# Top-k attention with a gated feed-forward on one core: the first eight units moved to a three-stage order with folded scores

## The chip, the cores and the metric

The kernel runs on one core of one Trainium2 chip. Its time is the device time of one execution in microseconds (us), the median of several runs. Five engines of the core matter here. PE is TensorE, the matrix engine (PEld is its loading of weights). DVE is VectorE, ACT is ScalarE, POOL is GpSimd. SP is the queue from which nearly all transfers are issued. Each engine works through its own instructions in program order and waits on the others through semaphores.

## The reference

There are 8 batches of 8 heads, 576 tokens and 64 elements per head. For each query only the 32 largest scores are kept. The result is put together to 4608 rows of 512, which go through a feed-forward with 2048 hidden elements.

```python
def _attn_ref(q, k, v):                       # q, k, v: (8, 8, 576, 64)
    scores = 1.0 / np.sqrt(D) * np.matmul(q, k.transpose(0, 1, 3, 2))
    kth = np.partition(scores, -32, axis=-1)[..., -32:-31]
    scores = np.where(scores >= kth, scores, -1000000000.0)
    scores = scores - np.max(scores, axis=-1, keepdims=True)
    attn = np.exp(scores)
    attn = attn / (np.sum(attn, axis=-1, keepdims=True) + 1e-09)
    return np.matmul(attn, v)

def _moe_ref(x, w_in, w_out):                 # w_in: (512, 2048), w_out: (2048, 512)
    h = x @ w_in
    g = h * np.cos(h)
    return g @ w_out
```

The two weight matrices arrive as 64-bit floats and the kernel turns them into 32-bit floats itself. This is called decoding here.

## The kernel before

The attention is cut into 144 units: 128 tokens and a pair of heads each. Four units in a row (the four pairs of heads) make a block of 128 tokens, ready for the feed-forward. The program is a loop over slots. In slot i unit i is searched for its 32 largest scores, while older units are at later stages. Weights come in 32 chunks of 512 KB: 16 of w_in, then 16 of w_out.

A chunk goes from a transfer to ACT, then to DVE, then to POOL:

```python
def decode_first(n):      # ACT: abs, sign, low word
    ...
        nc.scalar.activation(out=w, in_=hi.bitcast(F32), func=AF.Abs, scale=2.0**16)
        nc.scalar.sign(hi.bitcast(F32), hi)
        nc.scalar.mul(out=lo, in_=lo.bitcast(U32), mul=2.0**-29)
def decode_second(n):     # DVE: maximum, shift
    ...
        nc.vector.tensor_scalar(out=w, in0=w, scalar1=2.0, scalar2=None, op0=ALU.max)
        nc.vector.tensor_scalar(out=wi, in0=wi, scalar1=3, scalar2=None, op0=ALU.logical_shift_left)
def decode_third():       # POOL: add the low word, multiply by the sign
    ...
        nc.gpsimd.tensor_tensor(out=wi, in0=wi, in1=st[:, :, 0], op=ALU.add)
        nc.gpsimd.tensor_tensor(out=w, in0=w, in1=st[:, :, 1].bitcast(F32), op=ALU.mult)
```

A new chunk is loaded only while fewer than 8 chunks and live feed-forward tiles are held (`staged() + ff["live"] >= CHUNKS` stops it).

The search of a unit has two forms. Without folding, each of four rounds takes the eight largest of 576 scores for two heads (`max`), and three rounds remove them (`match_replace`). With folding, the scores are first split into the larger and the smaller of two halves (288 each). The larger halves get four rounds, the smaller ones two, and two small reductions in the next slot merge the results:

```python
def fold(u, op):                      # op is max, then min
    ...
    nc.vector.tensor_tensor(out=u["rest"][...], in0=sc[:, :, 0, 0:HS], in1=s[:, :, HS:S], op=op)
def topk_round(u, rnd):
    ...
    if u["folds"]:
        search(at, rest[:, :, 0:HS], rest[:, :, 0:HS], rnd < lasts)
        if rnd < TOPK // 16:
            search(low, rest[:, :, HS:S], rest[:, :, HS:S], rnd < TOPK // 16 - 1)
    else:
        search(at, u["s"] if rnd == 0 else rest, rest, rnd < lasts)
```

`sc` is the tile in PSUM in which `scores` leaves a unit's scores. There is one (`bufs=1`), and `transposes_now` uses the same. `take_scores` copies it to `s` on ACT.

The later stages: `bounds`, `mask` and `exponentials` (ACT), `reciprocal` (DVE), `normalise` (POOL), the transposes (on PE in the early slots, and then copied by ACT; by transfers later), `values` (PE) and `take_values` (ACT). The feed-forward runs beside them: `feed(n)` issues up to n steps on PE. A step needs credit (4.1 a slot, at most 5), finished values or gated tiles that are two ticks old (each `feed` is a tick), and decoded weights. `take_banks` copies finished PSUM banks (ACT). `reduce_first` and `reduce_second` reduce the argument of the cosine (POOL), `sines` evaluates it (ACT), `gate` multiplies (POOL).

The early slots are these:

```python
EARLY, LAST = 2 * NP, NU - NP         # 8, 140
u["folds"] = EARLY + 2 <= i < LAST + 2

def early_slot(i, u, w):              # u = unit i, w = unit i - 1
    n = 3 if i < 6 else 2
    topk_first(u, w)                  # merges of w, folds or first round of u
    decode_second(1 if i == 0 else n)
    scores(units[i + 1])
    for load, b, hp in at_slot.get(i, []):
        load(b, hp)
    load_weights(n)
    if w:
        bounds(w)
        mask(w)
        exponentials(w)
        reciprocal(w)
    topk_round(u, 1)
    if i == 0:
        decode_second(2)
    topk_round(u, 2)
    topk_round(u, 3)
    if w:
        normalise(w)
    take_banks()
    take_scores(units[i + 1])
    gate(1)
    decode_third()
    feed(2)
    reduce_first()
    reduce_second()
    if i != NP:
        decode_first(n - 1)
    if w:
        transposes_now(w)
    feed(1)
    decode_first(n - len(wq["second"]))
    if w:
        values([w])
        take_values([w])
    feed(2)
    sines(2)
```

`sines(2)` evaluates when two reduced tiles wait, or one has waited long enough. Slots 0 to 8 are such early slots; slots 9 to 140 have another order (`slot`), with the search first, then `decode_second(2)`, and with normalise, split, write and a transfer that transposes for units two and three slots old. The last four have an order of their own.

Of the kernel before, what the change touches and what calls it, by code (L numbers as in the profile page):

```python
# [31 lines left out]
def kernel(  # L32
# [16 lines left out]
    NP = H // 2  # L49
# [35 lines left out]
    for i in range(DF // CW):  # L85
        w = consts.tile([P, NC, CW], F32, tag=f"w_in{i}", name=f"w_in{i}")
# [16 lines left out]
    def load_weights(n):  # L103
        for _ in range(n):
            i = wq["next"]
            if i >= len(chunks):
                return
            src, dst = chunks[i]
            if not DECODE:
                nc.sync.dma_start(out=dst, in_=src)  # L110
                wq["next"] = wq["done"] = i + 1
                continue
            if staged() + ff["live"] >= CHUNKS:
                return
            st = ffw.tile([P, CW, 2], I32, tag="g", name="st", bufs=CHUNKS)
            nc.sync.dma_start(out=st.rearrange("p w i -> p (w i)"), in_=src)
            wq["loaded"].append((st, dst))
            wq["next"] = i + 1
# [87 lines left out]
    def scores(u):  # L206
        sc = u["sc"] = ps.tile([P, 2, 2, 512], F32, tag="sc", name="sc", bufs=1)
        for h in range(2):
            for j in range(2):
                d = slice(j * D, (j + 1) * D)  # L210
                for b, q0, rows, r0 in u["parts"]:
                    st = pairs[b, u["hp"]]
                    nc.tensor.matmul(  # L213
                        sc[r0 : r0 + rows, j, h, 0:HS],
                        st["q"][d, q0 : q0 + rows],
                        st["k"][d, h * HS : (h + 1) * HS],
                        start=True,
                        stop=True,
                    )

    def take_scores(u):
        s = u["s"] = work.tile([P, 2, S], F32, tag="s", name="s", bufs=4)
        nc.scalar.copy(  # L223
            out=s.rearrange("p j (h w) -> p (j h) w", h=2),
            in_=u["sc"].rearrange("p j h w -> p (j h) w")[:, :, 0:HS],
        )
        if not u["folds"]:
            del u["sc"]
# [23 lines left out]
    def topk_first(u, w):  # L252

        u["top"] = tops[u["n"] % len(tops)]
        merges = [merge_first, merge_second] if w and w["folds"] else []
        if u["folds"]:
            for op in (ALU.max, ALU.min):
                fold(u, op)
                if merges:
                    merges.pop(0)(w)  # L260
        else:
            u["rest"] = work.tile([P, 2, S], F32, tag="rest", name="rest", bufs=1)
        for merge in merges:
            merge(w)
        topk_round(u, 0)
# [38 lines left out]
    def bounds(u):  # L304

        ends = u.pop("top").rearrange("p j r i -> p j (r i)")
        ends = ends[:, :, 2 * TOPK - 2 :] if u["folds"] else ends[:, :, 2 * TOPK - 2 :: 2 - 2 * TOPK]
        nb = u["nb"] = small.tile([P, 2, 2], F32, tag="nb", name="nb")
        nc.scalar.mul(out=nb, in_=ends, mul=-SCALE)  # L309
        nd = u["nd"] = small.tile([P, 2], F32, tag="nd", name="nd")  # L310
        for j in range(2):
            nc.scalar.activation(  # L312
                out=nd[:, j : j + 1], in_=ends[:, j, 1:2], func=AF.Identity,
                bias=nb[:, j, 0:1], scale=SCALE,
            )

    def mask(u):

        s, nb = u["s"], u.pop("nb")
        for j in range(2):  # L320
            nc.scalar.activation(  # L321
                out=s[:, j], in_=s[:, j], func=AF.Prelu, bias=nb[:, j, 1:2], scale=SCALE, alpha=FAR
            )

    def exponentials(u):
        s, nd = u["s"], u.pop("nd")
        den = u["den"] = small.tile([P, 2], F32, tag="den", name="den")
        for j in range(2):
            nc.scalar.activation(  # L329
                out=s[:, j], in_=s[:, j], func=AF.Exp, bias=nd[:, j : j + 1], scale=1.0,  # L330
                accum_out=den[:, j : j + 1],
            )

        nc.scalar.activation(out=den, in_=den, func=AF.Identity, bias=eps, scale=1.0)

    def reciprocal(u):
        u["rden"] = small.tile([P, 2], F32, tag="rden", name="rden")
        nc.vector.reciprocal(u["rden"], u.pop("den"))  # L338

    def normalise(u):  # L340
        s, rden = u["s"], u.pop("rden")
        for j in range(2):
            nc.gpsimd.tensor_scalar(  # L343
                out=s[:, j], in0=s[:, j], scalar1=rden[:, j : j + 1], scalar2=1.0,
                op0=ALU.mult, op1=ALU.mult,
            )
# [123 lines left out]
    def take_banks():  # L470
        while full:
            take, *what = full.popleft()
            take(*what)
# [122 lines left out]

    EARLY, LAST = 2 * NP, NU - NP

    for i, u in enumerate(units):
        u["n"] = i
        u["folds"] = EARLY + 2 <= i < LAST + 2

    def early_slot(i, u, w):
        n = 3 if i < 6 else 2
        topk_first(u, w)
        decode_second(1 if i == 0 else n)
        scores(units[i + 1])
        for load, b, hp in at_slot.get(i, []):  # L610
            load(b, hp)
        load_weights(n)
        if w:
            bounds(w)
            mask(w)
            exponentials(w)
            reciprocal(w)
        topk_round(u, 1)
        if i == 0:
            decode_second(2)  # L620
        topk_round(u, 2)
        topk_round(u, 3)
        if w:
            normalise(w)
        take_banks()
        take_scores(units[i + 1])
        gate(1)
        decode_third()
        feed(2)
        reduce_first()  # L630
        reduce_second()
        if i != NP:
            decode_first(n - 1)
        if w:
            transposes_now(w)
        feed(1)
        decode_first(n - len(wq["second"]))
        if w:
            values([w])
            take_values([w])  # L640
        feed(2)
        sines(2)

    def slot(i, u, w, x, y, z):
        if x:
# [94 lines left out]
    for i in range(NU + 1):  # L740
        ff["end"] = i >= NU
        ff["credit"] = min(ff["credit"] + 4.1, 5.0)
        ff["now"] += 1
        wq["ready"] = wq["done"]
        u, w = (units[i - n] if 0 <= i - n < NU else None for n in range(2))
        x, y = (units[i - n] if EARLY <= i - n < LAST else None for n in range(2, 4))
        z = units[i - 5 : i - 3] if i % 2 and EARLY <= i - 5 < LAST else None
        if i <= EARLY:
            early_slot(i, u, w)
        elif i <= LAST:  # L750
            slot(i, u, w, x, y, z)
        else:
            last_slot(i, u, w, x, y, z)
# [47 lines left out]
```

## Time and profile before

| | before |
|---|---|
| time, median of 3 runs | 1527.04 us (1526.19 to 1527.17) |
| span of the profiled execution | 1522.8 us |
| PE busy | 1433.9 us (94%) |
| DVE busy | 1417.3 us (93%) |
| POOL busy | 1107.0 us (73%) |
| ACT busy | 1069.3 us (70%) |
| start of slots 0, 1, 6, 10, 15 | 7.94, 21.37, 86.24, 139.98, 195.98 us |

The profile is that of one execution. A line of it names the source line (L138), the engine, the operation, what it writes and reads, the shape, how often it came, its busy time and the mean duration in ns. After the last bar stands the idle time before it and what ended that. The view of stretches has the length of each stretch and then the busy time of each engine in it. The timeline has a start, a duration and one or several merged instructions per line. The start of a slot is read from the timeline as the first DVE instruction of its unit.

### The profile page before, as it was taken

How to read it: one execution, taken by the hardware profiler on the slowest of the kernel's cores; microseconds unless marked ns; L12 is line 12 of the kernel's file. 1: busy time of each engine (PE TensorE's matmuls, PEld its weight loads, DVE VectorE, ACT ScalarE, POOL GpSimd, SP SyncE). 2: the span in 40 equal slices, each digit the busy share in tenths (PEclk: the TensorE clock that was granted, in tenths of full speed). 3: DMA queues.
4: the chain of work that ended last, by engine and by line, in shares of the span. 5: the costliest groups of instructions: out<-in, count | busy, mean ns of one | idle time of the engine just before them, and what ended most of it. 6: DMA issues, size and time to landing. Idle time of an engine off the chain costs nothing.

```text
span 1522.8 us, 30130 instructions
## 1 busy us (share of the span) xinstructions
PE 1433.9 (94%) x10360; PEld 1023.1 (67%) x10360; DVE 1417.3 (93%) x4689; ACT 1069.3 (70%) x2120; POOL 1107.0 (73%) x838
## 2 busy tenths in 40 slices
PE   4577798999999999999999999999999999999998
PEld 3464466676767676767676767676767676767575
DVE  7999999999999999999999999999999999999721
ACT  7888667676767677767676777676777777776731
POOL 4777958777878787878787878777777777787600
PEclk6688899999999999999999999999999999999999
DMA  8432365536664655554665455645554456544200
GB/s 271 141 93 83 96 169 166 163 117 160 170 165 111 152 144 165 161 148 137 165 171 138 126 148 165 177 121 159 164 163 132 133 142 167 139 141 114 70 10 14
DMA packets 371754, 212.20 MB, mean 139 GB/s; under 512 B 321296, under 2 KB 337937, under 8 KB 371601
## 3 DMA queue, kind: packets, MB, share of 16 engines
q1 hardware_dynamic: 366192, 200.63, 48.0%
q10 hardware_dynamic: 5408, 9.65, 1.8%
q8 instruction: 81, 1.33, 0.4%
q14 instruction: 73, 0.59, 0.1%
HBM read 45.09 MB, written 87.29 MB: 87 GB/s over the span
## 4 chain that ended last, share of the span: by engine, by line
PE 70%; ACT 13%; DVE 10%; DMA 3%; issue 2%; SPq 1%; POOL 0%; ACTq 0%; POOLq 0%; DVEq 0%
PE mm L454 30%; PE o L530 23%; PE sc L213 8%; PE o L404 8%; DVE top L299 4%; DVE rest L302 3%; ACT s L329 2%; ACT x L511 2%; ACT s L321 2%; DMA pT<-rows 2%; ACT s L223 1%; ACT L511 1%; DVE rest L239 1%; DVE w_out L138 1%; ACT nd L312 1%
## 5 line engine op out<-in xcount | busy, mean ns | idle before, releaser
L299 DVE MAX8 top<-rest 128x8 f32<-128x288 f32 (+1 forms) x1656 | 682.2, 461 | 0.0
L454 PEld LDWEIGHTS mm<-xT,w_in 128*128 128x128 f32 x4608 | 545.0, 193 | 102.2 <-issue 91.8
L454 PE MATMUL mm<-xT,w_in 128*128 128x128 f32 x4608 | 565.2, 278 | 4.3 <-ACT xT L410 4.2
L530 PE MATMUL o<-w_out,g 128*128 128x512 f32 x1152 | 541.8, 603 | 4.0 <-POOL w_out L148 3.9
L302 DVE MATCH_REPLACE8 rest<-top,rest 128x288 f32<-128x288 f32 (+1 forms) x1104 | 495.5, 457 | 0.0
L530 PEld LDWEIGHTS o<-w_out,g 128*128 128x128 f32 x1152 | 203.8, 192 | 201.2 <-issue 193.0
L343 POOL TENSOR_SCALAR s<-s,rden 128x576 f32<-128x576 f32 x288 | 212.9, 751 | 139.3 <-DVE rden L338 139.3
L355 POOL COPY halves<-s 128x2304 uint16<-128x2304 uint16 x132 | 277.8, 2105 | 35.6 <-DMA rows<-halves 28.5
L329 ACT ACTIVATE s<-s,nd 128x576 f32<-128x576 f32 x288 | 220.7, 769 | 0.4
L223 ACT COPY s<-sc 128x1152 f32<-128x1152 f32 x144 | 160.7, 1116 | 84.9 <-PE sc L213 84.7
L321 ACT ACTIVATE s<-s,nb 128x576 f32<-128x576 f32 x288 | 205.4, 760 | 0.0
L213 PE MATMUL sc<-k,q 64*128 64x288 f32 (+1 forms) x1280 | 187.3, 443 | 19.0 <-ACT s L223 8.7
L239 DVE TENSOR_TENSOR rest<-sc,s 128x576 f32<-128x576 f32 x264 | 198.7, 753 | 4.9 <-DVE rden L338 0.4
L518 POOL TENSOR_TENSOR g<-g,x 128x1024 f32<-128x1024 f32 x68 | 161.4, 2375 | 51.6 <-ACT x L511 46.9
L309 ACT ACTIVATE nb<-top 128x4 f32<-128x4 f32 x144 | 29.1, 202 | 233.5 <-DVE top L292 233.2
L404 PE MATMUL o<-pT,v 128*64 128x128 f32 (+1 forms) x2560 | 166.0, 272 | 19.2 <-DMA pT<-rows 10.7
L404 PEld LDWEIGHTS o<-pT,v 128*64 128x64 f32 x2560 | 136.4, 141 | 65.1 <-issue 36.8
L501 POOL TENSOR_TENSOR x<-g,x 128x1024 f32<-128x1024 f32 x68 | 161.0, 2367 | 5.7
L213 PEld LDWEIGHTS sc<-k,q 64*128 64x128 f32 (+1 forms) x1280 | 102.2, 183 | 81.5 <-issue 22.5
L492 POOL TENSOR_SCALAR x<-g 128x1024 f32<-128x1024 f32 x68 | 71.3, 1049 | 89.7 <-ACT g L466 89.7
L466 ACT ACTIVATE g<-mm 128x512 f32<-128x512 f32 x144 | 82.1, 582 | 48.6 <-PE mm L454 48.6
L302 DVE MATCH_VALUE_LOAD rest<-top,rest 128x8 f32 x1104 | 86.4, 78 | 0.0
(52 smaller groups left out, 1014.8 us busy)
## 6 DMA issues: line engine op xcount, KB each, us to landing
rows<-halves SPq DMA_DIRECT2D x132, 576.0 KB, 3.2
out_dram<-ob ACTq DMA_DIRECT2D x36, 256.0 KB, 2.8
q<-in_q_dram SPq DMA_DIRECT2D x31, 288.0 KB, 3.0
st<-in_moe_w_in_dram SPq DMA_DIRECT2D x16, 512.0 KB, 5.2
v<-in_v_dram SPq DMA_DIRECT2D x32, 256.0 KB, 3.1
st<-in_moe_w_out_dram SPq DMA_DIRECT2D x16, 512.0 KB, 3.5
k<-in_k_dram SPq DMA_DIRECT2D x31, 144.0 KB, 3.4
k<-in_k_dram SPq DMA_DIRECT2D x32, 128.0 KB, 3.8
```

The lines of the kernel that those rows point to most:

```text
L213: nc.tensor.matmul(sc[r0 : r0 + rows, j, h, 0:HS], st["q"][d, q0 : q0 + rows], st["k"][d, h * HS : (h + 1) * HS], start=True, stop=True,)
L223: nc.scalar.copy(out=s.rearrange("p j (h w) -> p (j h) w", h=2), in_=u["sc"].rearrange("p j h w -> p (j h) w")[:, :, 0:HS],)
L239: nc.vector.tensor_tensor(out=u["rest"][:, :, i * HS : (i + 1) * HS], in0=sc[:, :, 0, 0:HS], in1=s[:, :, HS:S], op=op,)
L299: nc.vector.max(to[:, j], src[:, j])
L302: nc.vector.match_replace(rest[:, j], to[:, j], src[:, j], NEG)
L321: nc.scalar.activation(out=s[:, j], in_=s[:, j], func=AF.Prelu, bias=nb[:, j, 1:2], scale=SCALE, alpha=FAR)
L329: nc.scalar.activation(out=s[:, j], in_=s[:, j], func=AF.Exp, bias=nd[:, j : j + 1], scale=1.0, accum_out=den[:, j : j + 1],)
L343: nc.gpsimd.tensor_scalar(out=s[:, j], in0=s[:, j], scalar1=rden[:, j : j + 1], scalar2=1.0, op0=ALU.mult, op1=ALU.mult,)
L355: nc.gpsimd.tensor_copy(out=halves, in_=s.rearrange("p (k h) -> p h k", h=2))
L404: nc.tensor.matmul(o[d, to], lhsT, rhs, start=c == 0, stop=c == NT)
L454: nc.tensor.matmul(mm[:, at : at + w], w_in[f // FC][:, c, (f % FC) * P : (f % FC + 1) * P], blk["xT"][:, c], start=c == 0, stop=c == NC - 1,)
L530: nc.tensor.matmul(o, g[:, at : at + P], w_out[f], start=f == 0, stop=f == NF - 1)
```

## The change

Three things are done in the early slots. First, folding, which so far began with unit 10, is used from unit 0 on. Second, the stages are spread: what was done for unit i - 1 in one slot is now done for two units, the masking and exponentials for w = unit i - 1 and the reciprocal, normalisation, transposes and values for x = unit i - 2. The reciprocal stands at the start of the slot, so DVE needs no result of the same slot. The next scores are computed and copied after the transposes, since both use the one PSUM tile. The early order now runs through slot 9, so that units 0 to 7 still pass through it to their values. Third, slot 0 loads five chunks of weights instead of three, so that two more are on the chip ahead of their decoding. The loads now stand after `decode_third`, and the sines are evaluated when one tile waits instead of two.

```diff
     for i, u in enumerate(units):
         u["n"] = i
-        u["folds"] = EARLY + 2 <= i < LAST + 2
+        u["folds"] = i < LAST + 2
 
-    def early_slot(i, u, w):
+    def early_slot(i, u, w, x):
         n = 3 if i < 6 else 2
+        if x:
+            reciprocal(x)
         topk_first(u, w)
         decode_second(1 if i == 0 else n)
-        scores(units[i + 1])
-        for load, b, hp in at_slot.get(i, []):
-            load(b, hp)
-        load_weights(n)
-        if w:
-            bounds(w)
-            mask(w)
-            exponentials(w)
-            reciprocal(w)
         topk_round(u, 1)
         if i == 0:
             decode_second(2)
         topk_round(u, 2)
         topk_round(u, 3)
         if w:
-            normalise(w)
-        take_banks()
-        take_scores(units[i + 1])
+            bounds(w)
+            mask(w)
+            exponentials(w)
+        if x:
+            normalise(x)
+            transposes_now(x)
         gate(1)
         decode_third()
+        for load, b, hp in at_slot.get(i, []):
+            load(b, hp)
+        load_weights(n if i else n + 2)
+        decode_first(1)
+        feed(1)
+        scores(units[i + 1])
+        take_scores(units[i + 1])
+        if x:
+            values([x])
+            take_values([x])
+        take_banks()
         feed(2)
         reduce_first()
         reduce_second()
-        if i != NP:
-            decode_first(n - 1)
-        if w:
-            transposes_now(w)
-        feed(1)
         decode_first(n - len(wq["second"]))
-        if w:
-            values([w])
-            take_values([w])
         feed(2)
-        sines(2)
+        take_banks()
+        sines(1)
 ...
-        if i <= EARLY:
-            early_slot(i, u, w)
+        if i <= EARLY + 1:
+            early_slot(i, u, w, units[i - 2] if i >= 2 else None)
```

## The prediction

> **What bounds the kernel now.** I began with the page's 40 slices. Most of the span looks alike; only the first six or seven slices and the last two do not.
>
> ```profile
> PE   4577798999999999999999999999999999999998
> DVE  7999999999999999999999999999999999999721
> PEclk6688899999999999999999999999999999999999
> ```
>
> DVE is full from the second slice on. PE is half idle for some 200 us and full afterwards. So a gain or loss must come from the first 200 us. That start I cut at the first DVE instruction of each unit's search (slot 0 starts at 7.94 us, slot 15 at 195.98 us). The view of stretches gives, for slots 2, 5, 7, 10, 12 and 14 (time, PE, PEld, DVE, ACT, POOL, then clock and DMA):
>
> ```profile
> 34.81:47.01 12.20, 6.50 (x37) 4.82 (x35) 12.09 (x29) 11.13 (x25) 9.14 (x9) 0.64 0.50 163
> 71.93:86.24 14.31, 12.30 (x83) 10.50 (x85) 12.08 (x28) 13.79 (x29) 9.06 (x9) 0.78 0.54 165
> 98.09:111.91 13.82, 7.51 (x59) 5.84 (x59) 13.75 (x27) 10.92 (x24) 12.08 (x11) 0.77 0.22 71
> 139.98:151.82 11.84, 10.07 (x36) 5.35 (x36) 11.73 (x37) 9.09 (x18) 9.57 (x8) 0.86 0.30 100
> 163.68:177.00 13.32, 10.64 (x68) 6.21 (x68) 13.21 (x38) 7.88 (x14) 12.14 (x11) 0.75 0.51 133
> 186.49:195.98 9.49, 7.48 (x42) 3.73 (x42) 9.45 (x34) 5.18 (x12) 4.99 (x4) 1.00 0.62 194
> ```
>
> Early slots are DVE slots: DVE is busy for practically the whole slot, except where it waits for the denominators (slot 5, 2.1 us; slot 1, 1.3 us; the waits `DVE rden L338 <- ACT den L334` sum to 4.3 us before 200 us). PE waits for inputs there, and runs at 0.5 to 0.8 of its clock.
>
> Is there DVE time that is not work? The groups by line, before 200 us, say yes. The same shift of the same 128x512 shape has two means:
>
> ```profile
> L138 DVE TENSOR_SCALAR w_out<-w_out 128x512 int32<-128x512 int32 x16 | 16.6, 1038 | 0.5
> L138 DVE TENSOR_SCALAR w_in<-w_in 128x512 int32<-128x512 int32 x16 | 7.8, 487 | 0.5
> ```
>
> The timeline shows why. First slot 3, then slot 10:
>
> ```profile
> 50.22 0.43 DVE L138 TENSOR_SCALAR w_in<-w_in 128x512 int32<-128x512 int32 x1
> 51.02 0.43 DVE L138 TENSOR_SCALAR w_in<-w_in 128x512 int32<-128x512 int32 x1
> 51.82 0.43 DVE L138 TENSOR_SCALAR w_in<-w_in 128x512 int32<-128x512 int32 x1
> 52.94 1.47 POOL L343 TENSOR_SCALAR s<-s,rden 128x576 f32<-128x576 f32 x2 [3.27 <-DVE rden L338]
> ...
> 145.10 0.43 DVE L138 TENSOR_SCALAR w_out<-w_out 128x512 int32<-128x512 int32 x1
> 145.67 1.34 POOL L147 TENSOR_TENSOR w_out<-w_out,st 128x512 int32<-128x512 int32 x1 [1.74 <-ACT s L329]
> 145.90 1.40 DVE L138 TENSOR_SCALAR w_out<-w_out 128x512 int32<-128x512 int32 x1
> 147.09 1.36 POOL L148 TENSOR_TENSOR w_out<-w_out,st 128x512 f32<-128x512 f32 x1
> ```
>
> In slot 3 POOL stands still while DVE decodes, because its normalisation waits for the reciprocal, which DVE issues after the decode. In slot 10 POOL is free, takes the first decoded chunk 0.14 us after it is ready, and DVE's next shift takes 1.40 us instead of 0.43.
>
> **What the skill says.** The Trainium skill, "SBUF — State Buffer", section "Who interferes with whom": DVE in a two-port mode (`tensor_scalar` is one of the operations that can enter it) and GpSimd take a shared port pair for a whole instruction, and the other blocks. The trace agrees: 1.40 us is POOL's remaining 1.1 us plus the shift. By the same section PSUM-plus-SBUF folds and searches are free of it; their durations here do not move. "TensorE: Matmul & The Clock Gate", section "What's actually happening": PE runs at half clock after an idle window. Here the 20 value matmuls take 2.9 us in slot 3 and 1.3 us in slot 6, eight scores between 1.24 and 2.5. "ScalarE: Activation LUTs", section "What ACT_TABLE_LOAD costs": about 1283 ns a load; the trace has 1.28 us. Asking for one sine instead of two gives one or two more switches there and back, each 2.6 us of ACT.
>
> **Part 1: folding units 0 to 9.** Unfolded, in slot 2: four pairs of maxima 1.32 us apart and three pairs of replacements 1.45 apart, 4 x 1.32 + 3 x 1.45 = 9.63, with the reciprocal 9.73. Folded, slot 14: 9.49 in all (folds with merges 1.56, six pairs of maxima at 0.73, four pairs of replacements at 0.84, reciprocal 0.19). Only 0.24 us a unit, 2.4 us in ten. The halves are shorter but there are more of them.
>
> **Part 2: three stages instead of two.** The reciprocal of x = unit i-2 now opens the slot, its denominator being long done. The 4.3 us of waits go. But normalising, too, now runs in the first 1.8 us of a slot, so POOL is idle again when DVE decodes (4.9 us into the slot: 0.19 + 1.56 + first round 3.14). This is slot 10's situation, in every early slot.
>
> Cost of the decode with POOL awake. Two chunks: 147.22 - 144.65 = 2.57 us against 1.6 undisturbed. Three chunks, carrying slot 10's pattern on: the third maximum waits for POOL's L148 (ends 148.45), the third shift for POOL's next L147 (ends about 149.9); decode ends at about 150.1, so 5.45 us against 2.4.
> - Slots 1 to 5 (three chunks): 9.49 + 5.45 = 14.94 each, 74.7 in all. Before: 86.24 - 21.37 = 64.9. Loss 9.8.
> - Slot 0: the decodes in it already collided before (13.43 us). I find 12.5 of DVE work, but scores of unit 1 are now copied by ACT after chunk 3 is decoded; that chunk landed at 17.9 us, so the copy ends near 20.8. Slot 1 starts at 21.05, a gain of 0.3.
> - Slots 6 to 9 (two chunks), before 53.7: slots 6 and 7 9.49 + 2.57 = 12.06 each. In 8 and 9 POOL's range reduction from the slot before (three 1.05 and one 2.4 us) runs into the decode, as it did in slots 7 and 8 before; I put 12.5 and 13.6. Sum 50.2, gain 3.5.
> - Slots 10 to 12, before 37.0: a gate that used to come in slot 9 now comes in 10 and pushes normalise and split (1.5 and 2.1 us) onto the decode: 13.5; then 12.1 and 14.1. Sum 39.7, loss 2.7.
> - Slots 13 and 14 unchanged, 19.0.
> Total: +9.8 - 0.3 - 3.5 + 2.7 = +8.7 us at the start of slot 15.
>
> **Part 3: is the ACT order a second limit?** The copy of the next scores now stands behind the pT copies and one decode, and scores share their PSUM tile with the transposes. From slot start: merges 1.6, bounds to exponentials 3.8 (48.74 to 52.55), pT copies 1.2, a chunk 1.9, copy 1.0: 9.5 to 9.9, well inside 14.94. Then ACT waits for the values matmuls, cold until 11.7, and decodes two chunks to 15.8: still before the next merges at 16.5. Without collisions it would be ACT that holds slots 2 to 5 at about 14.1.
>
> **Part 4: two more chunks ahead.** Decoding stays at three per slot, then two, by the code's counts; only arrival is earlier. ACT's waits for landings, `DMA st<-in_moe_w_in_dram`, are 3.9 us before 200 us, all by 23 us and mostly off DVE's path. Worth 0 to 1 us.
>
> **Feed-forward supply.** I walked the queue rules slot by slot (credit 4.1 up to 5, two ticks after values and after gates, chunks ready). First steps run in slot 5 in both; units 4 to 7 are complete a slot later. Steps issued by the end of slot 9: 13 before, 12 after; of slot 12: 23 and 23; of slot 15: 31 and 31; identical from there to the end (544 of 576 by slot 144). So nothing is carried to the tail; slots 15 on are the same program, started later or earlier. The change in time is the shift of slot 15.
>
> **Rivals.**
> - *A gain of 5 to 10 us* (about 1519): POOL does not meet the decode, and slots 1 to 5 last 12.0 to 12.5. For it: 4.3 us of waits and 2.4 of folding truly vanish, and ACT was 93% busy but not late. Against it: only the wait for the reciprocal kept POOL away.
> - *ACT as the bound* (about 1531): collisions less than I think, slots 2 to 5 at 14.1 from cold values and the new order. The two causes overlap, so they do not add.
> - *A longer loss* (1545 or more): table switches, late normalisation and the shared PSUM tile delay the scores' copy in slots 7 to 10, where POOL is full; 2 to 3 us a slot.
> - *A late tail*: fewer feed-forward steps early. The counts speak against it.
>
> **Range and chances.** 1527.04 + 8.7 is 1536 us. Six us of slack below covers half the collisions being absent and some gain; ten above covers the third rival: 1521 to 1546. Two per cent is 30.5 us, which would need more than 2 us in each of 15 slots: same 0.97, faster 0.01, slower 0.02.
>
> **What would show it.** In the changed profile the w_in shifts (L138's counterpart) should average near 1 us instead of 487 ns, with POOL's adds beside them; early searches should start about 15 us apart in slots 1 to 5; waits of DVE for denominators should be gone; slot 15 should start near 205 us and everything after it take the same 1327 us. I am wrong if w_in shifts stay at 0.43 us, if DVE waits for copied scores (then ACT is the bound), or if the stretch from slot 15 to the end changes by more than 3 us.

## Result and the profile after

| | before | after |
|---|---|---|
| time, median of 4 runs each | 1527.11 us (1526.19 to 1527.98) | 1542.64 us (1542.26 to 1544.63) |
| ratio, 95% interval | | 1.0104 (1.0087 to 1.0122) |
| start of slots 1, 6, 10, 15, 21 | 21.37, 86.24, 140.16, 196.17, 253.55 us | 21.42, 96.05, 148.59, 207.45, 269.12 us |

The change costs 15.5 us. Here and below a slot starts with its first fold, or its first maximum where nothing is folded. By that measure the changed kernel is 11.3 us late at slot 15 and 15.6 us late at slot 21, as much as the medians differ. (The two profiled executions differ by more, 1542.8 against 1522.8 us.)

The 40 slices of the changed kernel. As before, the first seven and the last two hold nearly everything that is not full, and PE now has less in slices 1, 4 and 6:

```profile
PE   2575888999999999999999999999999999999999
DVE  7998998999999999999999999999999999999721
PEclk6586989999999999999999999999999999999999
```

The stretches of slots 2, 5, 7, 10, 12 and 14 in the changed kernel, cut at the first DVE instruction of each (length; then PE, PEld, DVE, ACT and POOL; clock, DMA share, GB/s). The last row is slots 15 to 20 together:

```profile
36.15:51.08 14.93, 6.62 (x37) 5.11 (x37) 14.79 (x41) 11.34 (x24) 9.51 (x8) 0.61 0.45 135
80.93:95.86 14.93, 10.16 (x69) 8.38 (x69) 14.79 (x41) 12.12 (x25) 9.52 (x8) 0.66 0.53 150
107.91:119.99 12.08, 9.81 (x94) 8.89 (x93) 11.97 (x38) 9.12 (x21) 7.52 (x7) 1.00 0.30 90
145.01:164.25 19.24, 19.20 (x103) 12.98 (x104) 13.11 (x39) 14.53 (x25) 12.64 (x10) 0.89 0.19 60
176.41:188.27 11.86, 6.22 (x66) 4.80 (x64) 11.75 (x39) 6.86 (x15) 11.46 (x9) 0.95 0.12 50
197.76:207.25 9.49, 6.87 (x14) 3.26 (x15) 9.45 (x34) 8.37 (x14) 9.36 (x7) 0.50 0.48 110
207.45:269.12 61.67, 55.56 (x456) 42.07 (x455) 56.93 (x198) 39.45 (x81) 37.98 (x31) 0.94 0.62 170
```

The same stretch of slots 15 to 20 in the kernel before:

```profile
196.17:253.55 57.38, 50.45 (x426) 39.66 (x423) 56.79 (x198) 41.83 (x84) 39.27 (x31) 0.91 0.66 173
```

Slots 2 and 5 take 14.93 us, and DVE is busy for 14.79 of them. That is DVE time, not a wait. The stretch of slot 10 is different: 19.24 us from the reciprocal that stands ahead of the first fold, DVE busy for 13.11. In slots 15 to 20 DVE does the same work in both kernels (56.93 and 56.79 us, 198 instructions), but the changed kernel takes 4.3 us longer for it, and PE has 5.1 us more to do there. By the groups of PE's instructions, 48 matmuls against w_out lie before slot 15 and 20 in slots 15 to 20 in the kernel before, 38 and 31 in the changed one: work that had not been done by slot 15 is done there.

The groups by line before 210 us in the changed kernel show what fills DVE. The w_in shifts now take as long as the w_out shifts (means in ns after the comma):

```profile
L138 DVE TENSOR_SCALAR w_out<-w_out 128x512 int32<-128x512 int32 x16 | 16.1, 1004 | 0.5
L138 DVE TENSOR_SCALAR w_in<-w_in 128x512 int32<-128x512 int32 x16 | 15.5, 971 | 0.6
```

The timeline of slot 3 in the changed kernel (start, duration, instruction) has what slot 10 of the kernel before had:

```profile
56.44 0.43 DVE L138 TENSOR_SCALAR w_in<-w_in 128x512 int32<-128x512 int32 x1
57.00 1.34 POOL L147 TENSOR_TENSOR w_in<-w_in,st 128x512 int32<-128x512 int32 x1 [4.21 <-ACT den L334]
57.23 1.39 DVE L138 TENSOR_SCALAR w_in<-w_in 128x512 int32<-128x512 int32 x1
58.42 1.36 POOL L148 TENSOR_TENSOR w_in<-w_in,st 128x512 f32<-128x512 f32 x1
58.55 1.51 DVE L137 TENSOR_SCALAR w_in<-w_in 128x512 f32<-128x512 f32 x1
59.74 1.47 POOL L147 TENSOR_TENSOR w_in<-w_in,st 128x512 int32<-128x512 int32 x1
60.10 1.40 DVE L138 TENSOR_SCALAR w_in<-w_in 128x512 int32<-128x512 int32 x1
```

The first shift is free. POOL then takes the chunk, and each later DVE step ends 0.28 to 0.29 us after a POOL instruction has ended. The releaser named at 57.00 is the profile's guess; POOL took the chunk 0.13 us after its shift ended (56.87).

DVE's largest waits before 260 us in the changed kernel (total, times, longest). Those for copied scores are 6.7 us at the very start and, new, 1.16 and 3.44 us at the ends of slots 8 and 9:

```profile
DVE rest L239 <- ACT s L223: 12.1, 4, 6.7
DVE rden L338 <- ACT den L334: 6.1, 5, 2.6
```

The timeline around slot 9 in the changed kernel shows how those come about:

```profile
135.83 2.36 POOL L501 TENSOR_TENSOR x<-g,x 128x1024 f32<-128x1024 f32 x1
136.38 1.28 ACT L511 ACT_TABLE_LOAD   x1
138.17 2.05 POOL L343 TENSOR_SCALAR s<-s,rden 128x576 f32<-128x576 f32 x2
140.79 1.28 ACT L329 ACT_TABLE_LOAD   x1
143.94 1.05 ACT L382 COPY pT<-tp 128x512 f32<-128x512 f32 x2
145.05 2.29 PE L213 MATMUL sc<-k,q 64*128 64x288 f32 x8 [3.44 <-ACT pT L382]
148.59 0.76 DVE L239 TENSOR_TENSOR rest<-sc,s 128x576 f32<-128x576 f32 x1 [3.44 <-ACT s L223]
```

ACT loads its table for one sine and loads it back (136.38 and 140.79), so its exponentials, its copies of the transposes and through the shared PSUM tile the next scores come late. POOL's normalisation stood behind the last step of a range reduction until 138.17. The scores then run cold, that is at PE's lower clock: 2.29 us, where the same eight take 1.24 us warm (in e11 below).

### The profile page after: what moved, and what is told of

It is laid out like the page before. It is cut to its first block, busy times and chain, and to the rows that moved or that the text cites. A ratio compares the mean times of both kernels' runs of the same rounds, so it can differ in the third digit from the quotient of the medians.

```text
span 1542.8 us, 30290 instructions
## 1 busy us (share of the span) xinstructions
PE 1431.3 (93%) x10360; PEld 1022.5 (66%) x10360; DVE 1425.2 (92%) x4809; ACT 1071.6 (69%) x2120; POOL 1110.0 (72%) x838
## 4 chain that ended last, share of the span: by engine, by line
PE 71%; ACT 12%; DVE 9%; DMA 3%; issue 2%; POOL 2%; SPq 1%; ACTq 0%; POOLq 0%; DVEq 0%
PE mm L454 30%; PE o L530 24%; PE sc L213 9%; PE o L404 8%; DVE top L299 3%; DVE rest L302 2%; DMA pT<-rows 2%; ACT x L511 2%; ACT s L329 2%; ACT s L321 2%; ACT L511 1%; ACT s L223 1%; DVE rest L239 1%; DVE w_in L138 1%; DMA st<-in_moe_w_in_dram 1%
## 5 line engine op out<-in xcount | busy, mean ns | idle before, releaser
L299 DVE MAX8 top<-rest 128x8 f32<-128x288 f32 x1716 | 690.9, 455 | 0.0
L302 DVE MATCH_REPLACE8 rest<-top,rest 128x288 f32<-128x288 f32 x1144 | 503.5, 451 | 0.0
L213 PE MATMUL sc<-k,q 64*128 64x288 f32 (+1 forms) x1280 | 191.5, 449 | 43.5 <-DVE top L292 23.8
L239 DVE TENSOR_TENSOR rest<-sc,s 128x576 f32<-128x576 f32 x284 | 213.8, 753 | 16.9 <-ACT s L223 12.1
L404 PE MATMUL o<-pT,v 128*64 128x128 f32 (+1 forms) x2560 | 163.4, 273 | 11.2 <-DMA pT<-rows 11.2
L302 DVE MATCH_VALUE_LOAD rest<-top,rest 128x8 f32 x1144 | 94.9, 83 | 0.0
```

Of the source, the lines that this page charges most:

```text
L213: nc.tensor.matmul(sc[r0 : r0 + rows, j, h, 0:HS], st["q"][d, q0 : q0 + rows], st["k"][d, h * HS : (h + 1) * HS], start=True, stop=True,)
L239: nc.vector.tensor_tensor(out=u["rest"][:, :, i * HS : (i + 1) * HS], in0=sc[:, :, 0, 0:HS], in1=s[:, :, HS:S], op=op,)
L299: nc.vector.max(to[:, j], src[:, j])
L302: nc.vector.match_replace(rest[:, j], to[:, j], src[:, j], NEG)
L404: nc.tensor.matmul(o[d, to], lhsT, rhs, start=c == 0, stop=c == NT)
```

## Experiments

Each run is set against runs of the kernel before on the same chip. The table has the sums of slot lengths and two starts, all in us, and the ratio to the kernel before.

| kernel | slots 1–5 | 6–9 | 10–14 | slot 15 at | 15–20 | slot 21 at | ratio (95%) |
|---|---|---|---|---|---|---|---|
| before | 64.87 | 53.92 | 56.01 | 196.17 | 57.38 | 253.55 | 1 |
| after | 74.63 | 52.54 | 58.86 | 207.45 | 61.67 | 269.12 | 1.0104 (1.0087–1.0122) |
| e1 after, last chunk first | 63.46 | 54.46 | 59.72 | 198.74 | 61.31 | 260.05 | 1.0054 (1.0038–1.0071) |
| e2 after, two sines | 74.61 | 50.26 | 67.80 | 213.96 | 57.71 | 271.67 | 1.0127 (1.0110–1.0144) |
| e3 before, last chunk first | 65.65 | 52.94 | 58.73 | 197.58 | 57.63 | 255.21 | 1.0008 (1.0000–1.0017) |
| e4 before, folds | 81.44 | 67.73 | 57.55 | 227.01 | – | – | 1.0200 (1.0184–1.0216) |
| e5 after, no folds | 75.62 | 53.07 | 56.32 | 206.56 | 61.62 | 268.18 | 1.0109 (1.0091–1.0126) |
| e6 before, two loads | 65.14 | 53.93 | 56.30 | 196.44 | 57.53 | 253.97 | 0.9997 (0.9988–1.0006) |
| e7 e1, values copied later | 59.49 | 55.87 | 59.85 | 195.93 | 61.66 | 257.59 | 1.0014 (1.0005–1.0023) |
| e9 e7, one bank copy | 59.49 | 54.24 | 59.18 | 193.59 | 61.01 | 254.60 | 1.0008 (0.9999–1.0018) |
| e10 after, less reduction | 74.61 | 49.71 | 59.08 | 204.68 | 59.82 | 264.50 | 1.0059 (1.0044–1.0074) |
| e11 e9, reduction earlier | 59.51 | 51.32 | 62.75 | 194.93 | 59.18 | 254.11 | 0.9992 (0.9985–0.9999) |
| e12 e11, less reduction | 59.51 | 46.55 | 57.81 | 184.29 | 58.25 | 242.54 | 0.9936 (0.9920–0.9952) |
| e13 before, less reduction | 65.38 | 50.35 | 54.96 | 192.14 | 57.30 | 249.44 | 0.9969 (0.9959–0.9978) |

e10, e12 and e13 leave out work: most of the range reduction of the cosine's argument in the first two blocks. They measure what that work costs and are no candidates.

### e1: POOL takes the last decoded chunk first

DVE finishes chunks 1, 2, 3 in a row. If POOL takes chunk 3 first, it can't begin while DVE decodes, and nothing else of the program changes.

```diff
 def decode_third():
-            st, w = wq["third"].popleft()
+            st, w = wq["third"].pop()
```

> The changed kernel (1542.6 us), with GpSimd's third decode step taking a slot's chunks last first, so that it begins only when VectorE has decoded all of them and the two never meet there. Nothing else is changed. Theory 1 (the port that GpSimd holds is what makes slots 1 to 5 last 14.9 us): the mean w_in shift goes from 971 to about 430 ns, slots 1 to 5 shrink to about 12.0 us, slots 6 to 12 by 0.5 to 1 each: 1520 to 1528 us. Theory 2 (the new ScalarE order holds these slots at about 14.1 us as soon as the collisions are gone, because it waits for the values matmuls at half clock and then decodes two chunks): shifts fall to 430 ns all the same, but slots 2 to 5 stay at 13.5 to 14.3 us with VectorE waiting for copied scores: 1533 to 1538 us. Theory 3 (the port has nothing to do with it): 1541 to 1544 us.

1533.28 us (1532.03 to 1536.97), 9.4 below the changed kernel, or 8.2 when each is taken against the kernel before on its own chip. The w_in shifts average 427 ns instead of 971. Slots 1 and 2 take 11.89 and 11.88 us, slot 3 12.69, slots 4 to 6 about 13.5. Stretches of slots 2 and 4 in e1:

```profile
32.99:44.87 11.88, 6.61 (x37) 5.17 (x37) 11.74 (x39) 9.84 (x21) 9.11 (x9) 0.50 0.54 166
57.56:71.07 13.51, 6.04 (x41) 4.13 (x39) 11.74 (x39) 11.66 (x24) 9.94 (x9) 0.63 0.41 119
```

DVE works for 11.74 us in both; slot 4 is longer by a wait. The timeline of e1 from slot 4 to 5 names it:

```profile
58.71 0.27 ACT L410 COPY xT<-o 128x128 f32<-128x128 f32 x1 [1.18 <-PE o L404]
...
69.92 1.12 ACT L223 COPY s<-sc 128x1152 f32<-128x1152 f32 x1 [0.39 <-PE sc L213]
71.07 0.76 DVE L239 TENSOR_TENSOR rest<-sc,s 128x576 f32<-128x576 f32 x1 [1.67 <-ACT s L223]
```

ACT stands at the copy of cold values, is late with everything behind it, and the next search waits 1.67 us for its scores. So the collision is the cause of 14.9 us slots, and ACT's order is a second bound at 13.5 behind it. That 11.2 us gained over slots 1 to 5 became 9.1 at slot 21, because slots 6 to 14 gave 2.8 back.

### e2: sines in twos again

```diff
         take_banks()
-        sines(1)
+        sines(2)
```

> The changed kernel with one number put back: its early slots ask for two waiting tiles before they evaluate sines, as before. Theory 1 (the early single sine costs a table switch in ScalarE's order in slots 8 and 9, which delays the copy of the scores in slots 9 to 11, and its order of feed-forward steps leaves PE four steps behind at slot 13, which shows as 4.3 us lost in slots 16 to 20): the lag at slot 15 falls from 11.3 us by 2 to 4, and the stretch of slots 15 to 21 returns to its old length: 1534 to 1538 us. Theory 2 (late normalisation behind the range reduction on GpSimd causes the waits, the sines are incidental): 1540 to 1543 us, with the waits for copied scores in slots 9 and 10 still there.

1544.77 us (1544.48 to 1545.60): no gain. Slot 9 fell from 15.44 to 13.16 us, and slots 15 to 20 lost their excess, but slots 11 and 14 rose to 14.71 and 15.78. The timeline of e2 at the end of slot 14:

```profile
200.09 9.42 PE L530 MATMUL o<-w_out,g 128*128 128x512 f32 x16 [6.55 <-POOL g L518]
213.85 0.17 DVE L338 RECIPROCAL rden<-den 128x2 f32<-128x2 f32 x1 [6.29 <-ACT den L334]
```

PE stood 6.55 us before a tile that POOL had not gated yet, then ran 16 matmuls, the first of them cold. Scores stood behind those, exponentials behind the scores, and DVE waited 6.29 us for a denominator. So the first theory is right about slot 9 and about slots 15 to 20, but not about the time: the lag comes out at another place. In this kernel four steps of the feed-forward, which the changed kernel runs after unit 15's scores, stand ahead of them again, as in the kernel before (see the next part).

### e3: the kernel before, last chunk first

The edit of e1 in the kernel before, in which the two decode steps meet in slots 0, 9, 10 and 12.

> The kernel before (1527.1 us) with GpSimd's third decode step taking a slot's chunks last first. Theory 1 (the port): in the kernel before collisions between the two decode steps occur only in slots 0, 9, 10 and 12, about 1 us each, so slots shorten by 3 to 4 us in sum: 1523 to 1525 us. Theory 3 (no effect of the port): 1526.5 to 1528 us.

1526.70 us (1524.91 to 1529.75), no gain. Slots 0, 9, 10 and 12 are each about 1 us shorter (12.37, 13.46, 10.87, 12.32), but slots 1, 11 and 14 are 0.8, 1.6 and 3.1 us longer. In slot 14 PE again waits for a gate, 3.95 us, and DVE for a denominator, 3.08. The 4 us of DVE time saved did not reach slot 21.

### e4: the kernel before with folds

```diff
-        u["folds"] = EARLY + 2 <= i < LAST + 2
+        u["folds"] = i < LAST + 2
```

> The kernel before with folding from unit 0 on and nothing else changed. By the sum of instructions a folded unit takes 0.24 us less of VectorE than an unfolded one, ten units 2.4 us: 1524 to 1526 us. Rival (folding holds the PSUM tile of scores until the second fold, and adds merges that the bounds of the unit wait for, so ScalarE starts later in slots where the reciprocal is awaited in the same slot): 1528 to 1534 us, with more waiting of VectorE for denominators.

1555.99 us (1554.31 to 1558.21): 30 us worse, far outside what either theory had. Slots 2 to 9 take 16.4 to 19.6 us. Timeline of e4 in slot 3 (49.30 to 65.70):

```profile
51.00 1.09 PE L378 MATMUL tp<-ident,s 128*128 128x128 f32 x4 [8.46 <-DVE top L292]
...
56.92 0.21 ACT L309 ACTIVATE nb<-top 128x4 f32<-128x4 f32 x1
...
60.84 0.17 DVE L338 RECIPROCAL rden<-den 128x2 f32<-128x2 f32 x1 [4.36 <-ACT den L334]
```

Folds read the scores in PSUM during the search, so the tile comes free late, and the transposes of the unit before wait for it (8.46 us). A folded unit's bounds need its merges in the next slot, and its denominator is awaited in that same slot (4.36 us here, 35.5 in all before 260 us). In the order of two stages, folding early costs 30 us; in that of three it does not (e5). The parts of the change depend on each other.

### e5: the changed kernel without folds

The line of e4, put back in the changed kernel.

> The changed kernel (1542.6 us) with folding again only from unit 10 on; the three-stage order and the loads stay. Theory 1 (in the new order folding is worth only its VectorE time): VectorE needs 9.73 + 5.45 = 15.2 us in slots 1 to 5 instead of 14.9, so +1 to +3: 1543 to 1546 us. Theory 2 (holding the PSUM tile of scores through the folds, which made folding cost 30 us in the old order, costs here too, in slots 9 to 11): without it the copies of scores come earlier and the time falls to 1536 to 1541 us.

1543.09 us (1540.47 to 1546.15), the same as with folds. Slots 1 to 5 are 15.12 us instead of 14.93, so folding is worth 0.2 us a unit as computed. What slots 1 to 9 lose by this (1.5 us) comes back in slot 10 (13.40 instead of 15.76).

### e6: the kernel before with two more chunks ahead

```diff
-        load_weights(n)
+        load_weights(n if i else n + 2)
```

> The kernel before (1526 to 1527 us) with five instead of three chunks loaded in slot 0 and nothing else. Theory 1 (decoding, not landing, sets the pace): no more than 1 us less, 1525.5 to 1527.5 us, with ScalarE's waits for landed w_in chunks falling from 3.9 us. Rival (the extra megabyte delays the q, k and v transfers behind it): 1528 to 1532 us, with PE or VectorE waiting for transfers in slots 1 to 3.

1525.23 us (1523.98 to 1527.65). No effect that can be measured. ACT's waits for landed w_in chunks did not fall either (3.9 us before 200 us in the kernel before, 5.1 here).

### e7: e1, and a chunk decoded before the values are copied

```diff
         if x:
             values([x])
+        decode_first(1)
+        if x:
             take_values([x])
```

> The changed kernel with the third decode step last first (that alone gave 1533.3 us) and with one chunk decoded on ScalarE between the values matmuls and their copy, so that ScalarE no longer idles 1.2 us for them. Theory 2 of the first such run (ScalarE's order is the bound of slots 3 to 6 once the collisions are gone): slots 3 to 6 fall from 12.7 to 13.6 us to 12.0 to 12.4, the waits of VectorE for copied scores there vanish, and the time is 1527 to 1530 us. Rival (the lag that is gained is paid back in slots 9 to 20, where PE and GpSimd are behind): slots 3 to 6 shrink all the same, but 1532 to 1534 us.

1527.39 us (1524.30 to 1533.53). Slots 1 to 5 are now all 11.88 to 11.94 us: ACT decodes while the cold values run, and both bounds are gone there. But slots 6 and 7 grew to 14.18 and 16.04. Timeline of e7 from slot 6 to 8:

```profile
98.32 0.60 ACT L466 ACTIVATE g<-mm 128x512 f32<-128x512 f32 x1 [1.99 <-PE mm L454]
101.96 0.60 ACT L466 ACTIVATE g<-mm 128x512 f32<-128x512 f32 x1 [3.04 <-PE mm L454]
102.45 0.20 ACT L309 ACTIVATE nb<-top 128x4 f32<-128x4 f32 x1
...
110.43 0.76 DVE L239 TENSOR_TENSOR rest<-sc,s 128x576 f32<-128x576 f32 x1 [3.83 <-ACT s L223]
```

The second `take_banks()`, at the end of the slot, makes ACT wait for feed-forward sums of the same slot (1.99 and 3.04 us). Bounds come after it, and so, in the end, the next scores (3.83).

### e9: e7 with one bank copy a slot

```diff
         feed(2)
-        take_banks()
         sines(1)
```

> The kernel of the run before (last first, values copied late, 1527.4 us) without the second copying of PSUM banks that the change put at the end of an early slot. Theory (ScalarE waits there 1.4 to 4.2 us for feed-forward matmuls that PE has just begun, in front of the next unit's bounds, and this is what makes slots 6 and 7 last 14.2 and 16.0 us once the collisions are gone): slots 6 and 7 fall to 11.1 to 12 us, six us in sum, and if nothing behind gives it back the time is 1520 to 1523 us. Rival (slots 8 to 20 are held by the feed-forward itself, whose steps come later without that copy): slots 6 and 7 fall, slots 9 to 20 grow, 1525 to 1528 us.

1526.95 us (1525.27 to 1531.13). Slots 6 and 7 fell to 11.82 and 11.91, 6.5 us less, but slot 8 took 16.32. The timeline of e9 has POOL's last reduction step at 110.01 to 112.40, normalisation behind it, and then:

```profile
113.36 1.11 PE L378 MATMUL tp<-ident,s 128*128 128x128 f32 x4 [9.47 <-POOL s L343]
```

With ACT out of the way it is POOL's queue that holds the transposes, and so the scores behind them. But waiting is the smaller part: DVE is busy for 14.3 of the 16.32 us, against 11.0 of 11.09 in e7, because the reduction's steps now meet the decode (a maximum takes 2.56 us, a shift 1.15).

### e10: the changed kernel with less range reduction

```diff
 def reduce_first():
         gp = nc.gpsimd
+        if blk["t0"] < 2 * P:          # first two blocks: one step instead of three
+            gp.tensor_scalar(out=x, in0=g, scalar1=0.01, scalar2=0.0, op0=ALU.mult, op1=ALU.add)
+            return
 def reduce_second():
-        if not ff["end"]:              # and no subtraction
+        if not ff["end"] and blk["t0"] >= 2 * P:
```

> The changed kernel with most of the range reduction left out for the first two blocks of the feed-forward (one of GpSimd's four instructions is kept, about 1.05 of 5.6 us a tile, four tiles; the argument is scaled down instead). Theory (GpSimd, which carries the reduction of a slot over into the next one ahead of its normalisation, is what delays transposes, copied scores and gates in slots 8 to 12): the waits for copied scores in slots 9 and 10 (1.2 and 3.4 us) shrink below 1 us, slot 10 from 15.8 to 13 to 14 us, and the time to 1535 to 1538 us. Rival (ScalarE's table switches are what delays them): no more than 2 us less, 1540.5 to 1542.5 us.

1534.97 us (1533.73 to 1537.14), 7.7 us below the changed kernel, or some 6 when each is taken against the kernel before on its own chip. By lengths of single instructions (three of 1.05, one of 2.4), 4 tiles x 4.5 = 18 us of POOL are left out. Slots 8 and 9 are 12.05 and 13.54; slots 15 to 18 take 9.5 each; slot 10 stays at 15.72. So POOL's lag made all the loss in slot 8 (slots 6 and 7 take 12.06 too), nearly all of the wait at the end of slot 9 (0.16 us here, 3.44 in the changed kernel), and part of what is lost in slots 15 to 20. Slot 9 gains only 1.9 us because its decode now meets a gate: DVE is busy for 13.3 us of it instead of 11.9.

### e11: e9 with the reduction ahead of the third decode step

```diff
         gate(1)
+        reduce_first()
+        reduce_second()
         decode_third()
 ...
         feed(2)
-        reduce_first()
-        reduce_second()
```

> Last first, values copied late, one bank copying, and the range reduction moved on GpSimd from the end of a slot to behind normalisation and gate of the next, where GpSimd otherwise waits for the decode. Theory (late normalisation is what lengthens slots 8 to 10): normalisation starts in the first 0.5 us of these slots, transposes and scores follow, slots 9 and 10 fall to 11 to 13.5 us, though the reduction's last instruction now meets the decode once in a slot (about 2 us in up to four slots); 1518 to 1523 us. Rival (the meeting costs what the earlier normalisation brings): as the run with one copy, within 2 us.

1524.31 us (1520.69 to 1526.79) against 1525.49 of the kernel before on the same chip: the only complete kernel here whose interval lies below the kernel before, and barely: 0.08% (0.01 to 0.15%). Slot 14 starts 6.8 us earlier than in the kernel before (179.84), and then takes 15.09 us. Timeline of e11 in that slot:

```profile
178.52 2.34 POOL L518 TENSOR_TENSOR g<-g,x 128x1024 f32<-128x1024 f32 x1
180.92 9.57 PE L530 MATMUL o<-w_out,g 128*128 128x512 f32 x16 [4.05 <-POOL g L518]
190.42 1.24 PE L213 MATMUL sc<-k,q 64*128 64x288 f32 x8
191.76 1.12 ACT L223 COPY s<-sc 128x1152 f32<-128x1152 f32 x1 [8.18 <-PE sc L213]
194.83 0.17 DVE L338 RECIPROCAL rden<-den 128x2 f32<-128x2 f32 x1 [5.60 <-ACT den L334]
```

This is the chain of e2: gate, cold matmuls, scores, copy, denominator. PE takes its work in order, so scores that DVE needs soon stand behind feed-forward that waits for POOL.

### e12 and e13: less range reduction in e11 and in the kernel before

The edit of e10 in both.

> The kernel of the run with one copy and early reduction (1524.3 us; its slot 14 starts 6.8 us earlier than in the kernel before, but lasts 15.1 us, and slots 19 and 20 last 10.5 and 10.7), with most of the range reduction of the first two blocks left out as in the run on less reduction. Theory 1 (GpSimd's lag in slots 9 to 14, which makes PE stand in front of a gated tile, is what gives the gain back): slots 9 to 12 fall below 13 us, slot 14 to 9.5 us, and the time to 1514 to 1519 us. Theory 2 (PE has too much feed-forward to do in slots 13 to 20, whenever GpSimd delivers): slot 14 shortens, but slots 15 to 20 grow to 10 to 11 us each, and slot 21 starts no earlier than 250 us: 1521 to 1524 us.

1516.14 us (1513.03 to 1517.75). Slot 14 takes 9.50 us, slots 15 to 19 too, and slot 21 starts 11.6 us before that of e11. The waits of DVE's reciprocal, 6.1 us in the changed kernel for ACT's denominators and 1.2 put down to POOL, are 1.2 us in e12, all put down to POOL.

> The kernel before (1525.5 us) with the same part of the range reduction left out. Theory 1 (GpSimd's lag): slots 7 to 9, in which the reduction's last instruction stands in front of the decode (2.5 us each), shrink by 5 to 7 us in sum, slot 12 by 1 to 2 us, and all of it reaches the end: 1517 to 1521 us. Theory 2 (PE): the slots shrink as much, but slots 13 to 20 take most of it back: 1523 to 1526 us.

1519.93 us (1518.92 to 1524.61). Slots 7 and 8 are 12.13 and 11.93 us (13.82 before), and the 4.1 us are still there at slot 21. Stretch of slot 8 in e13:

```profile
110.81:122.74 11.93, 7.31 (x44) 5.48 (x40) 11.31 (x26) 10.30 (x23) 7.59 (x8) 0.64 0.29 91
```

POOL is busy for 7.59 us of it; slot 7 of the kernel before, also one of 13.8 us, had 12.08. DVE's own busy time fell as well, from 13.75 to 11.31 us, so the gain here is again a collision that is gone and no wait. Slot 7 of the kernel before, where the last step of the reduction meets the decode:

```profile
101.58 2.39 POOL L501 TENSOR_TENSOR x<-g,x 128x1024 f32<-128x1024 f32 x1
101.81 2.45 DVE L138 TENSOR_SCALAR w_out<-w_out 128x512 int32<-128x512 int32 x1
```

Less work for POOL thus acts in two ways. In e10's slots 8 and 9 waits go. In e13's slots 7 and 8 collisions go. In e12 it is both: slots 8 and 9 are 4.8 us shorter than in e11, all of it DVE's busy time, and slot 14 is 5.6 us shorter by a wait. Time saved on DVE in the early slots (e1, e3, e7, e9) was partly or wholly taken back; what less work for POOL saved (e10, e12, e13) is there at the end.

## Why the prediction was right, and where not

The time was put 8.7 us higher and came 15.5 us higher. Of the 6.8 us between, 2.6 lie before slot 15 and 4.3 in slots 15 to 20. Sums of slot lengths, and what each adds to the start of slot 15 (for slots 15 to 20, to that of slot 21):

| | before | predicted | after | predicted shift | shift |
|---|---|---|---|---|---|
| slot 0 (start of slot 1) | 21.37 | 21.05 | 21.42 | -0.3 | +0.05 |
| slots 1–5 | 64.87 | 74.7 | 74.63 | +9.8 | +9.8 |
| slots 6–9 | 53.92 | 50.2 | 52.54 | -3.5 | -1.4 |
| slots 10–12 | 37.02 | 39.7 | 39.87 | +2.7 | +2.9 |
| slots 13, 14 | 18.99 | 19.0 | 18.99 | 0 | 0 |
| slots 15–20 | 57.38 | unchanged | 61.67 | 0 | +4.3 |

**Part 2, the collision: right, and shown.** 14.94 us a slot were predicted, 14.91 to 14.94 came. A single change of POOL's order took it away (e1): shifts back to 427 ns, slots 1 and 2 to 11.89. This is what the Trainium skill, "SBUF — State Buffer", section "Who interferes with whom", says of the shared port pair: the blocked engine waits for the whole instruction. In slot 3 the decode of three chunks took 5.43 us (55.98 to 61.41), where 5.45 was put, instead of 2.4. One reading was a little off: the 1.40 us of the shift in slot 10 are POOL's remaining 1.11 us plus 0.29, not plus a whole shift of 0.43.

**Part 1, folding: right** for the changed kernel (e5, 0.2 us a slot). The prediction did not consider what folding does without the staging (e4, +30 us).

**Part 3, ACT's order: right as a second bound,** 13.5 us in slots 4 to 6 of e1 (slots 2 and 3 took 11.88 and 12.69), where 14.1 was put for slots 2 to 5. The rival "ACT as the bound" had 1531 us for a kernel without full collisions; e1 took 1533.28. ACT was busy for 91% of slots 1 to 5 in the kernel before, not 93. PE's clock, given as 0.5 to 0.8 for the early slots, was 1.00 and 0.99 in slots 6 and 9. **Part 4: right** in the time (e6), though the waits for landing did not shrink.

**Slots 8 and 9: mis-sized, and by another cause,** 12.5 and 13.6 put, 12.98 and 15.44 measured. I let the reduction run into the decode, which would be DVE time. But DVE is busy for only 11.7 and 11.9 us of them, and the rest is waiting. The third rival, "table switches, late normalisation and the shared PSUM tile", came true in small, at 1.2 + 3.4 us of waits for copied scores. Two loads of 1.28 us around one sine agree with the load time in the Trainium skill, "ScalarE: Activation LUTs", section "What ACT_TABLE_LOAD costs". The drain of some 1380 ns that it adds to each switch does not show beside the load at 136.38: the instruction before it ended at 136.36, and the sine began at 137.68. Such a pair stood in slot 9 of the kernel before too (126.00 and 132.44), and up to slot 15 the changed kernel has seven loads against six. With sines in twos slot 9 is 2.3 us shorter (e2), with less reduction 1.9 (e10).

**Slots 10 to 12: right in sum by luck.** 13.5, 12.1 and 14.1 were put, 15.76, 12.25 and 11.86 came. In slot 10 the late gate (154.32 to 156.73) held a shift for 2.47 us, and DVE waited 2.6 us for a denominator.

**"Slots 15 on are the same program, started later or earlier": wrong.** From slot 15 to the end the profiled executions take 1326.7 us before and 1335.4 after, where 3 us was the mark; 4.3 us of it lie in slots 15 to 20. The step that failed is the feed-forward supply. Its counts of steps issued by the ends of slots 12 and 15 (23 and 23, 31 and 31) agree with PE's order in the traces, but equal counts there were taken for the same program, and between those points the order differs. Between the scores of units 14 and 15 the kernel before runs 20 matmuls against w_out (a step has 4 of them), the changed kernel runs 4, and 12 follow only after the scores of unit 15. First the kernel before, then the changed one:

```profile
181.10 10.39 PE L530 MATMUL o<-w_out,g 128*128 128x512 f32 x20
...
192.38 2.67 PE L530 MATMUL o<-w_out,g 128*128 128x512 f32 x4
202.67 7.78 PE L530 MATMUL o<-w_out,g 128*128 128x512 f32 x12 [0.73 <-POOL g L518]
```

Ahead of unit 15's scores there are 48 such matmuls before and 32 after, ahead of unit 16's 48 and 44, ahead of unit 17's 56 in both. So by slot 15 PE had started 38 of them and not 48, and in slots 15 to 20 it is busy with them for 14.7 us instead of 9.4. From the waits of DVE in slots 15 to 20 of the changed kernel:

```profile
DVE rden L338 <- ACT den L334: 3.5, 4, 1.5
DVE rden L338 <- POOL x L493: 1.2, 1, 1.2
```

These 4.7 us of the reciprocal's waits, 0.4 us in the same slots of the kernel before, are the payback. One of them in the timeline of the changed kernel, slot 17:

```profile
224.11 1.12 ACT L223 COPY s<-sc 128x1152 f32<-128x1152 f32 x1 [2.36 <-PE sc L213]
...
227.19 0.17 DVE L338 RECIPROCAL rden<-den 128x2 f32<-128x2 f32 x1 [0.56 <-ACT den L334]
```

Scores come late from PE, the copy waits 2.36 us, exponentials follow, and DVE waits. All runs divide by the order: where 32 matmuls stand ahead of unit 15's scores (the changed kernel, e1, e5, e7, e9, e10), slots 15 to 20 take 59.8 to 61.7 us; where 48 do (the kernel before and the others), 57.3 to 59.2. In e2 sines in twos brought the old order back, so in the changed kernel the single sines had moved the four steps; the forecast had counted only their table switches. The old order is not better by itself: in e2, e3 and e11 PE and then DVE wait in slot 14 instead. That POOL's lag has a part in it is shown by e10, which keeps the changed kernel's order: slots 15 to 18 take 9.5 us again with nothing but POOL's work reduced. No run changed the order alone, so how the 4.3 us divide between order and lag is not shown. The rest of the excess in slots 19 and 20 of e10 (2.8 us above 9.5 each) is not explained.

**The rival "a gain of 5 to 10 us" had its slots right and its time wrong.** It foresaw slots of 12.0 to 12.5 us with the collision gone. e7 and e9 reach 11.9, 5.4 us less than before in slots 1 to 5, and yet are not faster than the kernel before (1.0014 and 1.0008). What lies between is POOL: its reductions and gates run into the decode later on, and scores and matmuls wait for it. e10, e12 and e13 show what both cost together.

Still open: how slots 9 and 10 divide exactly among table switches, normalisation and gate; and a further 4.4 us between slot 21 and the end that the profiled execution of the changed kernel has over that of the kernel before. The medians differ by 15.5 us only. The profiled execution of the changed kernel was the longest of its four (a span of 1542.8 us against 1540.0 to 1540.6), that of the kernel before took 1524.63 us, below its median of 1527.11, so most of the 4.4 us is a trait of these two executions.

## What to carry to other kernels

When a wait is removed, ask what it kept apart: here DVE's wait for denominators had also kept GpSimd out of DVE's decode, and without it the decode doubled; letting the second engine take the newest piece first keeps the two apart and took 3 us off such a slot, though it brought nothing in a kernel whose later slots gave the time back (e3). A gain in an early stage counts only if the slowest queue behind it (here GpSimd's reductions and gates, and the in-order matmuls that wait for them) is also earlier. Where two programs are said to be the same from some point on, compare the order of the work and what has been executed, and not only counts of what has been issued at chosen points. Test whether a stage's gain arrives by taking work off the suspected engine before building a better order for the others.

## What the runs showed of the hardware that was not expected

- Once GpSimd is in, DVE doesn't run ahead: in slot 3, shift, maximum and shift of 0.43 us each alternate with GpSimd's adds and multiplies of 1.34 to 1.47 us and take 1.39, 1.51 and 1.40 us. A few instructions of the faster engine then run at the pace of the slower.
- Sixteen w_out matmuls after a wait took 9.42 to 9.57 us (e2, e11), 0.6 us each, with load-to-load distances of 0.86 us at first and 0.43 at the end of the same group. Waiting for a gate thus cost PE its wait of 4 to 6.5 us and some 2.7 us of slow matmuls (9.57 - 16 x 0.43).
